# Hourglass attention and an ELU layer pair: zero matmuls through batch 0, 128-column denominator weights, and a one-element GpSimd read after each cast

## The chip, the cores and the metric

The kernel runs on one NeuronCore of a Trainium2 chip. The metric is the device time of one execution in microseconds (us). The profiled time, called the span, runs from the first to the last instruction of the program; the device time of the same execution is a little longer. Engines are named as in the profile: PE is TensorE (PEld its weight loads), DVE is VectorE, ACT is ScalarE, POOL is GpSimd, SP is SyncE, which here only issues DMAs. A suffix q (SPq, POOLq) means the engine's own instruction queue.

## The reference

Inputs are q, k and v of 8 batches x 8 heads x 576 positions x 64 in float32, and two weight matrices, w_in (512 x 2048) and w_out (2048 x 512). Each head's output is the sum of two attentions:

```python
q_d = q.reshape(B, H, Sd, 4, D).mean(axis=3)           # Sd = 144; k_d, v_d likewise
out_up = np.repeat(sm_attn(q_d, k_d, v_d), 4, axis=2)  # coarse: all 144 x 144
mask = np.abs(pos[:, None] - pos[None, :]) < 4         # local: a band of 7 keys
scores = np.where(mask, scale * q @ k.T, -1e9)
out = out_up + softmax(scores) @ v
```

The heads of a batch are put beside each other, which gives 4608 tokens of 512 values. Then h = x @ w_in, g = h where h > 0 and exp(h) - 1 elsewhere, and the result is g @ w_out, 4608 x 512 in float32.

## The kernel before

**Units.** A *pair* (b, j) is two heads of batch b, four pairs to a batch, 32 in all. A *token tile* t is 512 tokens, nine in all; a batch gives 576 tokens, so its end reaches into the next tile.

**One pair of attention.** `transposes` brings q and k to a head-dimension-first layout on PE; ACT (`evict_q` L281/L283, `evict_k` L296) copies them to SBUF. The sums over groups of four positions are made by `sums`: by DVE reductions in batch 0 (L305), by two POOL additions each in batch 1 (L311, L313), and by TensorE as part of the transposing matmul from batch 2 on. `masked_scores` (batches 0 and 1; the mask is added by a matmul, L334, then L340) or `scores` (L351, later batches) gives the local scores for six blocks of 96 queries by 112 keys, `coarse` (L361) the 144 x 144 ones. ACT exponentiates both (`pex` L372, `dex` L377). From batch 2 on, DVE multiplies by the mask (`mex`, L387). No maximum is subtracted.

**Denominators.** They are sums over keys, which lie on partitions, so they are made by matmuls with 0/1 weights. For batches 0 to 2 `den_some` does it for one or two pairs: pair i of the call writes rows 32i to 32i+31 of a PSUM bank, with 32-column weights at column position 32i (L443 seeds the bank so that no row is zero, L449 adds twelve local sums of 96 columns, L457 four coarse ones of 144). `reciprocals` inverts on DVE (L466), `spread_pe` (L476) copies each row to 64 partitions by matmul, and `spread_copy` (L485, L486) moves that to SBUF (`rcb`). Later batches do all four pairs at once (`denominators`) and spread through DRAM (`rd`).

**Output of a pair.** `outputs` (L501, L507) multiplies by v and by the four-position means of v (`vd`, by `v_first` in batches 0 and 1); `normalise` applies the reciprocals on DVE (gn L517, ln L520) and adds the two parts into the token tile xt (L529), on POOL, or for some early pieces on DVE.

**The two layers.** `mm1(t, fc)` makes 128 rows of h for a tile by four 128x512 matmuls (L545), ACT takes the exponential (`e`, L550), DVE clips it (`e`, L551) and joins it with the positive part (`gt`, L554). `mm2` multiplies by w_out (L565), ACT copies (L571), SP writes out.

**Loads and casts.** q and k of batches 0 and 1 are loaded by POOL-issued DMAs that convert to 16 bits (L152), as are w_in (WI, L139, in five column blocks) and w_out (WO, L143). q and k of later batches and all of v come by SP in float32 (L170, L193) and POOL casts them (`cast_qk` L183, `cast_v` L230); from batch 3 on POOL also makes vd from a second copy of v (`group_v`, L237 and L241).

**The order of the work.** It is written by hand. `first_batch` lists batch 0 step by step. Everything after is a list of events, `at(time, function, ...)`, sorted by time and recorded in that order; a unit of this time is one mm1/mm2 step, sixteen to a token tile. Each engine then runs its own instructions in the recorded order, and semaphores follow from the data. So a late instruction holds up all that is behind it on its engine. The numbers `base`, `tr` (transposes), `sc_` (scores), `dn` (denominators), `sp` (spreads) and `o0` (outputs) place the steps of a batch.

**PSUM.** In batch 0 there are three two-bank buffers (`two`: scores, rb, lg) and two one-bank buffers (`one`: tq, tk, vs, den, junk). Afterwards there are two of each kind: `two`, `misc` and `hp`. A tile takes the next buffer that is free, and its first writer waits for the last reader of the tile before.

**Zero matmuls.** `keep(t, n)` (L583) multiplies a zero tile by itself n times, 512 columns each, into a PSUM tile that is later overwritten. Before the change it is called twice: 14 times at the very start and twice in batch 0.

## Time and profile before

| | us |
|---|---|
| median of 3 runs (403.49 to 405.85) | 405.17 |
| the profiled execution | 404.46 |
| its span | 402.7 |
| PE busy / DVE / ACT / POOL | 369.8 / 270.3 / 206.9 / 174.4 |
| mean granted TensorE clock | 0.936 |

Busy PE is not PE at its peak: at a granted clock of 0.5 the same matmul takes about twice the time. Batch 0's attention alone fills the first 40 us. Batch 1's runs beside the first layer of token tile 0 until about 82 us; the other batches run beside the layers of tiles 1 to 7, until about 330 us. From there to the end there is only layer work. The chain that ended last is given as start, duration and what held the end of the program up at that time; in lines of the timeline the bracket at the end is the idle time of the engine before the instruction and what ended it. In lines by stretch the columns are the stretch, its length, then busy time and number of instructions of PE, PEld, DVE, ACT and POOL, the granted clock, the DMA share and GB/s.

### The profile page before, as it was taken

The page shows a single profiled execution, that of the slowest core. Times are in us where ns is not written, and L with a number is a line of the kernel's source. Part 1 is how long each engine was busy: PE and PEld are TensorE (multiplying, and loading weights), DVE is VectorE, ACT ScalarE, POOL GpSimd, SP SyncE. Part 2 cuts the span into 40 slices and gives each one's busy share as a digit, 9 for nine tenths or more (in the row PEclk, how much of TensorE's full clock was granted, in tenths as well). Part 3 has the DMA queues.
Part 4 walks back from the last instruction along what each step waited for, and adds up shares of the span by engine and source line. Part 5 has one row for each costly group of instructions (what it writes and reads, how often), then busy time and mean ns, then how long its engine had stood idle before and what let it go on. Part 6 is the DMA issues. An engine that isn't in the chain of part 4 may idle for free.

```text
span 402.7 us, 8286 instructions
## 1 busy us (share of the span) xinstructions
PE 369.8 (92%) x3244; PEld 194.6 (48%) x3244; DVE 270.3 (67%) x461; ACT 206.9 (51%) x386; POOL 174.4 (43%) x225
## 2 busy tenths in 40 slices
PE   7988999789896879988999999889999999999995
PEld 3766555445453435544544454445544444444442
DVE  3444387746747788679879886998897685555510
ACT  3442587147474456646654764566466434444321
POOL 4542872397402991089219922991490050000000
PEclk9555799989989689999999999999999999999999
DMA  8992999999976498569945994695300410100112
GB/s 137 192 208 52 145 181 145 178 163 228 201 149 116 99 188 172 137 121 227 199 127 108 222 220 131 120 234 154 77 28 28 107 55 26 48 32 26 55 52 78
DMA packets 125620, 51.99 MB, mean 129 GB/s; under 512 B 104156, under 2 KB 120974, under 8 KB 125582
## 3 DMA queue, kind: packets, MB, share of 16 engines
q1 hardware_dynamic: 116938, 44.56, 53.6%
q0 software_dynamic: 8048, 6.56, 10.9%
q8 instruction: 25, 0.41, 0.5%
q10 hardware_dynamic: 596, 0.35, 0.4%
q14 instruction: 13, 0.11, 0.1%
HBM read 48.21 MB, written 9.81 MB: 144 GB/s over the span
## 4 chain that ended last, share of the span: by engine, by line
PE 64%; DVE 18%; ACT 5%; POOL 4%; DMA 4%; issue 3%; SPq 0%; DVEq 0%; ACTq 0%; POOLq 0%
PE hp L545 24%; PE op L565 23%; DVE e L551 9%; DVE gt L554 4%; DVE ln L520 3%; PE sc L351 2%; ACT e L550 2%; POOL xt L529 2%; DMA k<-in_k_dram 2%; PE tk L269 1%; PE sc L340 1%; PE lg L501 1%; DVE mex L387 1%; DMA rd<-rc 1%; PE sc L361 1%
## 5 line engine op out<-in xcount | busy, mean ns | idle before, releaser
L545 PE MATMUL hp<-xt,WI 128*128 128x512 f16 x576 | 152.0, 389 | 4.9 <-DVE gt L554 4.8
L565 PE MATMUL op<-WO,gt 128*128 128x512 f16 x576 | 147.0, 383 | 0.7 <-DVE k L169 0.7
L550 ACT ACTIVATE e<-hp 128x512 f16<-128x512 f32 x144 | 86.2, 599 | 104.0 <-PE hp L545 100.7
L551 DVE TENSOR_SCALAR e<-e 128x512 f16<-128x512 f16 x144 | 80.1, 556 | 54.6 <-ACT e L550 53.7
L554 DVE SCALAR_TENSOR_TENSOR gt<-hp,e 128x512 f16<-128x512 f32 x144 | 99.6, 692 | 5.4
L529 POOL TENSOR_TENSOR xt<-ln,gn 128x64 f16<-128x64 f16 (+7 forms) x61 | 40.6, 693 | 131.3 <-DVE ln L520 131.3
L545 PEld LDWEIGHTS <-WI 128*128 128x128 f16 x576 | 54.0, 99 | 69.0 <-issue 11.4
L565 PEld LDWEIGHTS <-gt 128*128 128x128 f16 x576 | 54.6, 98 | 64.5 <-issue 2.7
L372 ACT ACTIVATE pex<-sc 112x576 f16<-112x576 f32 x64 | 41.4, 647 | 29.6 <-PE sc L361 19.9
L387 DVE TENSOR_TENSOR mex<-pex,MASK 112x1152 f16<-112x1152 f16 x24 | 24.7, 1030 | 14.6 <-ACT pex L372 14.6
L230 POOL CAST v<-v 112x768 f16<-112x768 f32 x32 | 27.2, 850 | 10.0 <-DMA v<-in_v_dram 10.0
L571 ACT COPY os<-op 128x512 f32<-128x512 f32 x36 | 21.2, 589 | 18.5 <-PE op L565 18.5
L237 POOL TENSOR_TENSOR v<-v 72x512 f32<-72x512 f32 x20 | 27.9, 1394 | 1.9 <-DMA v<-in_v_dram 1.8
L283 ACT CAST qt<-tq 128x720 f16<-128x720 f32 x24 | 18.1, 756 | 18.5 <-PE tq L324 11.2
L377 ACT ACTIVATE dex<-sc 72x288 f16<-72x288 f32 x64 | 25.4, 404 | 2.4 <-PE sc L361 2.4
L520 DVE TENSOR_TENSOR ln<-lg,rcb 128x576 f16<-128x576 f32 x32 | 23.9, 746 | 0.0
L183 POOL CAST k<-k 96x768 f16<-96x768 f32 x24 | 19.9, 831 | 1.4 <-DMA k<-in_k_dram 1.4
L183 POOL CAST q<-q 96x768 f16<-96x768 f32 x24 | 19.9, 829 | 1.0 <-PE tq L269 1.0
L351 PE MATMUL sc<-qt,kt 64*112 64x96 f16 x288 | 13.8, 221 | 6.4 <-DVE kd L315 4.0
L241 POOL TENSOR_TENSOR vd<-v 72x256 f16<-72x256 f32 x20 | 18.9, 943 | 1.6
L351 PEld LDWEIGHTS <-kt 64*112 64x112 f16 x288 | 10.0, 130 | 16.7 <-issue 8.4
L269 PE MATMUL tq<-QI,q 96*128 96x120 f16 x144 | 12.4, 226 | 5.3 <-POOL q L183 3.0
(83 smaller groups left out, 312.3 us busy)
## 6 DMA issues: line engine op xcount, KB each, us to landing
v<-in_v_dram SPq DMA_DIRECT2D x30, 336.0 KB
out_dram<-os SPq DMA_DIRECT2D x36, 256.0 KB
q<-in_q_dram SPq DMA_DIRECT2D x24, 288.0 KB
k<-in_k_dram SPq DMA_DIRECT2D x24, 288.0 KB
v<-in_v_dram SPq DMA_DIRECT2D x20, 288.0 KB
rcb<-rd SPq DMA_DIRECT2D x10, 288.0 KB
WO<-in_moe_w_out_dram POOLq DMA_DIRECT2D x4, 512.0 KB, 7.7
WI<-in_moe_w_in_dram POOLq DMA_DIRECT2D x3, 512.0 KB, 9.4
```

The source lines that it names most:

```text
L183: nc.gpsimd.tensor_copy(out=x[:], in_=t[:].rearrange("p (e c) d -> p c e d", e=2))
L237: nc.gpsimd.tensor_tensor(out=g[:, :, :, 0 : 2 * D], in0=g[:, :, :, 0 : 2 * D], in1=g[:, :, :, 2 * D :], op=AB.add,)
L351: nc.tensor.matmul(sc[e][0:KW, a : a + QB], s["kt"][r, QB * c : QB * c + KW], s["qt"][c][r], start=True, stop=True,)
L372: nc.scalar.activation(out=h2(s["pex"][:, e, :]), in_=g2(sc[0:KW], 0, HB), func=AF.Exp, scale=SCALE)
L387: nc.vector.tensor_tensor(out=s["mex"][:], in0=s["pex"][:], in1=mk2, op=AB.mult)
L520: nc.vector.tensor_tensor(out=h2(ln[:]), in0=g2(lg[:], 0, HB), in1=h2(rcb[:, j, 0:S]), op=AB.mult)
L529: eng.tensor_tensor(out=xt(t)[:, j, t0 - TBLK * t : t1 - TBLK * t], in0=ln[:, a:z], in1=_rep4(gn[:, a // 4 : z // 4]), op=AB.add,)
L545: nc.tensor.matmul(hp[:], WI[:, dc, 128 * fc : 128 * fc + 128], x[:, dc, :], start=(dc == 0), stop=(dc == DMC - 1),)
L550: nc.scalar.activation(out=e[:], in_=hp[:], func=AF.Exp)
L551: nc.vector.tensor_scalar(out=e[:], in0=e[:], scalar1=1.0, scalar2=-1.0, op0=AB.min, op1=AB.add)
L554: nc.vector.scalar_tensor_tensor(out=gts[t][:, fc, :], in0=hp[:], scalar=0.0, op0=AB.max, in1=e[:], op1=AB.add)
L565: nc.tensor.matmul(op_[:], gts[t][:, fc, 128 * tt : 128 * tt + 128], WO[:, fc, :], start=(fc == 0), stop=(fc == FCN - 1),)
```

## The change

Five things are changed.

1. **Zero matmuls in batch 0.** Forty 512-column zero matmuls are put between the steps of `first_batch`, in place of the two that were there: three ahead of the scores of pair 0 and four behind them, four and three behind `coarse` of pairs 0 and 1, four each between the q and the k transposes of pairs 2 and 3, three ahead of the outputs of pair 0, three ahead of `coarse` of pair 3, two each ahead of the outputs of pairs 1 to 3, and six at the end. The tiles that they write (score, rb, vs, den, lg) are allocated earlier for it.
2. **128-column weights in `den_some`.** IND and SEED are laid out anew, so that each matmul has 128 weight columns: all but one are zero in IND, and the matmuls of one pair add zeros to the rows of the other. Pairs follow each other instead of alternating. This is for batches 0, 1 and 2.
3. **`apart`.** After each cast of q, k and v of batches 2 to 7 POOL copies one element of the result into a 1x1 tile: 72 instructions.
4. **Batch 1 in another order.** Denominators are made for pairs 0 and 1 (step 7.6), 2 (11.7) and 3 (14.6) instead of for 0 and 1 (9.6), 2 and 3 (14.6). Spreads and outputs of a pair follow at once: outputs at 10.6, 11.6, 13.7 and 15.55 instead of two at 15.1 and two at 15.65. The sums of pair (1,0) are made by DVE reductions instead of POOL additions.
5. **Around batch 2's start.** Its first transposes come at -0.3 instead of 0, the casts for them 0.3 ahead instead of 0.2, and the first three loads of later q, k and v at steps 11.2, 12.2 and 13.2 instead of 11.2, 13.2 and 15.2.

In the order of each engine's instructions the rest follows from this: on POOL the casts of pair (2,0) stand before the last xt addition of batch 1, the cast of v of (1,1) and the first two WO loads one group of sums earlier; on PE one mm2 group stands behind the first transposes of batch 2 instead of ahead.

```diff
 RUNS = 2
+I1, I4 = 47, 176
 VG = 3
...
     vr[PAD + np.arange(QB), 48 + np.arange(QB) // 4] = 0.25
-    ind = np.zeros((128, 2, 63), dtype=f16)
-    ind[:, 0, 31] = 1.0
-    ind[:, 1, 31] = 4.0
-    ind = ind.reshape(128, 126)
-    seed = np.zeros((2, 64 + SD + HB), dtype=f16)
-    seed[0, 14:32] = 1.0
-    seed[1, 0:12] = 1.0
-    seed[0, 38:64] = 1.0
-    seed[1, 36:38] = 1.0
-    seed[0, 64:] = 1.0
-    seed[1, 64 + QB : 64 + SD] = 1.0
-    seed[1, 64 + 2 * SD :] = 1.0
+    ind = np.zeros((128, I4 + 63), dtype=f16)
+    ind[:, I1] = 1.0
+    ind[:, I4 + 31] = 4.0
+    seed = np.zeros((2, 288 + SD + HB), dtype=f16)
+    for n in range(2):
+        seed[0, 128 * n : 128 * n + 128] = 1.0
+        for i in range(n + 1):
+            seed[0, 128 * n + 32 * i : 128 * n + 32 * i + 14] = 0.0
+            seed[1, 128 * n + 32 * i : 128 * n + 32 * i + 12] = 1.0
+    seed[0, 262:288] = 1.0
+    seed[1, 260:262] = 1.0
+    seed[0, 288:] = 1.0
+    seed[1, 288 + QB : 288 + SD] = 1.0
+    seed[1, 288 + 2 * SD :] = 1.0
     sel = np.zeros((2, 32, 7, 2, 64), dtype=f16)
...
+    AP_ = sb.tile([1, 1], FP16, tag="apart", bufs=1, name="apart")
+    def apart(x):
+        nc.gpsimd.tensor_copy(out=AP_[:], in_=x)
     def cast_qk(b, j):
...
             nc.gpsimd.tensor_copy(out=x[:], in_=t[:].rearrange("p (e c) d -> p c e d", e=2))
+            apart(x[0:1, 0, 0, 0:1])
             got.append(x)
...
         nc.gpsimd.tensor_copy(out=v16[:], in_=v32[:].rearrange("p (e c) d -> p c e d", e=2))
+        if b >= RUNS:
+            apart(v16[0:1, 0, 0, 0:1])
         v16s[(b, j)] = v16
...
-    def transposes(b, j):
+    def transposes(b, j, fill=None):
...
             s[name] = t
+            if fill and name == "tk":
+                fill()
             for c in range(NB):
...
         src = s["q"][:, 0:S] if x == "q" else s["kt"][:, PAD : PAD + S]
-        if b == 0:
+        if b == 0 or (b, j) == (1, 0):
             nc.vector.tensor_reduce(
...
         den = bank("misc", "den")
-        o4 = 94 if b >= VG else 31
+        o4 = I4 + 31 if b >= VG else I1
         for j in range(NPAIR):
             nc.tensor.matmul(
-                den[32 * j : 32 * j + 32, 0:HB], C["SEED"][:, 32:64], C["SEED"][:, 64 + SD :],
+                den[32 * j : 32 * j + 32, 0:HB], C["SEED"][:, 256:288], C["SEED"][:, 288 + SD :],
                 start=True, stop=False, tile_position=(0, 32 * j),
...
                     nc.tensor.matmul(
-                        den[32 * j : 32 * j + 32, 0:HB], C["IND"][0:KW, 31 - r : 63 - r],
+                        den[32 * j : 32 * j + 32, 0:HB], C["IND"][0:KW, I1 - r : I1 + 32 - r],
                         st[(b, j)]["mex"][:, e, HB * g : HB * g + HB],
...
-        for i in range(len(js)):
-            nc.tensor.matmul(
-                den[32 * i : 32 * i + 32, 0:SD], C["SEED"][:, 0:32], C["SEED"][:, 64 : 64 + SD],
-                start=True, stop=False, tile_position=(0, 32 * i),
-            )
-        for r in range(12):
-            for i, j in enumerate(js):
+        n = 128 * len(js) - 128
+        nc.tensor.matmul(
+            den[:, 0:SD], C["SEED"][:, n : n + 128], C["SEED"][:, 288 : 288 + SD],
+            start=True, stop=False,
+        )
+        for i, j in enumerate(js):
+            for r in range(12):
+                a = I1 - 32 * i - r
                 nc.tensor.matmul(
-                    den[32 * i : 32 * i + 32, 0:QB], C["IND"][0:KW, 31 - r : 63 - r],
+                    den[:, 0:QB], C["IND"][0:KW, a : a + 128],
                     st[(b, j)]["mex"][:, r // 6, QB * (r % 6) : QB * (r % 6) + QB],
-                    start=False, stop=False, tile_position=(0, 32 * i),
+                    start=False, stop=False,
                 )
-        for e in range(2):
-            for kg in range(2):
-                for i, j in enumerate(js):
+            for e in range(2):
+                a = I1 - 32 * i - 12 - e
+                for kg in range(2):
                     nc.tensor.matmul(
-                        den[32 * i : 32 * i + 32, 0:SD], C["IND"][0:KG, 19 - e : 51 - e],
-                        st[(b, j)]["dex"][:, e, kg, :], start=False,
-                        stop=(e == 1 and kg == 1), tile_position=(0, 32 * i),
+                        den[:, 0:SD], C["IND"][0:KG, a : a + 128], st[(b, j)]["dex"][:, e, kg, :],
+                        start=False, stop=(j == js[-1] and e == 1 and kg == 1),
                     )
...
-    def v_first(b, j, copy=dve):
+    def v_first(b, j, copy=dve, vs=None):
-        vs = bank("misc", "vs") if late else one("vs")
+        vs = vs or (bank("misc", "vs") if late else one("vs"))
         v_sums(b, j, vs[0:KG], 128)
...
-        def T(j):
-            transposes(b, j)
+        def T(j, fill=None):
+            transposes(b, j, fill)
             evict_q(b, j, act)
...
-        def scored(j):
+        def tiles(j):
             SC[j] = [two("sc"), two("sc")]
+        def scored(j):
             for e in range(2):
...
-        def dens(js):
-            den = one("den")
+        def dens(js, den=None):
+            den = den or one("den")
             den_some(b, js, den)
...
-        def spread(j, copy):
-            rb = two("rb")
+        def spread(j, copy, rb=None):
+            rb = rb or two("rb")
             spread_pe(b, j, rb)
...
             lg = two("lg")
+            keep(lg, 2)
             outputs(b, j, lg)
...
         then()
+        tiles(0)
+        keep(SC[0][0], 3)
         scored(0)
+        tiles(1)
+        keep(SC[1][0], 4)
         T(1)
         coarsed(0)
-        keep(one("junk"), 2)
+        keep(SC[1][0], 4)
         scored(1)
-        T(2)
+        tiles(2)
+        T(2, lambda: keep(SC[2][0], 4))
         coarsed(1)
+        keep(SC[2][0], 3)
         v_first(b, 0)
...
         dens((0, 1))
-        T(3)
+        rb0 = two("rb")
+        T(3, lambda: keep(rb0, 4))
         coarsed(2)
-        spread(0, dve)
+        spread(0, dve, rb0)
         lg0 = two("lg")
+        vs = one("vs")
+        keep(vs, 3)
         outputs(b, 0, lg0)
-        v_first(b, 1)
+        v_first(b, 1, dve, vs)
+        tiles(3)
         scored(3)
         normalise(b, 0, lg0)
+        den = one("den")
+        keep(den, 3)
         coarsed(3)
         spread(1, act)
-        dens((2,))
+        dens((2,), den)
         ends(1)
...
         ends(3)
+        keep(one("junk"), 6)
         load_wi(1024, 1536)
...
-    def pair_outputs(b, j0):
-        lgs = [two("lg"), two("lg")]
-        for i in range(2):
-            outputs(b, j0 + i, lgs[i])
-        for i in range(2):
-            normalise(b, j0 + i, lgs[i])
+    def pair_outputs(b, js):
+        lgs = [two("lg") for _ in js]
+        for j, lg in zip(js, lgs):
+            outputs(b, j, lg)
+        for j, lg in zip(js, lgs):
+            normalise(b, j, lg)
...
             base, tr, sc_ = 0, (-0.1, 2.3, 6.3, 10.3), (0.3, 4.3, 8.3, 12.3)
-            dn, sp, o0 = (9.6, 14.6), (10.7, 13.6, 15.35, 15.45), (15.1, 15.65)
+            dn = ((7.6, (0, 1)), (11.7, (2,)), (14.6, (3,)))
+            sp, o0 = (8.7, 9.6, 12.8, 15.4), (10.6, 11.6, 13.7, 15.55)
         elif b == 2:
-            base, tr, sc_ = 16, (0, 3, 6, 9), (1.5, 4.5, 7.5, 10.5)
-            dn, sp, o0 = (8, 12), (9.2, 10.8, 12.6, 12.9), (13.3, 14.5)
+            base, tr, sc_ = 16, (-0.3, 3, 6, 9), (1.5, 4.5, 7.5, 10.5)
+            dn = ((8, (0, 1)), (12, (2, 3)))
+            sp, o0 = (9.2, 10.8, 12.6, 12.9), (13.3, 13.3, 14.5, 14.5)
         else:
...
             if b >= RUNS:
-                lead = 0.2 if (b, j) == (2, 0) else 3
+                lead = 0.3 if (b, j) == (2, 0) else 3
                 at(base + tr[j] - lead - 0.1, cast_qk, b, j)
...
         if b < 3:
-            for i in range(2):
-                at(base + dn[i], dens, b, (2 * i, 2 * i + 1))
+            for t, js in dn:
+                at(base + t, dens, b, js)
             for j in range(NPAIR):
                 at(base + sp[j], spread, b, j, act if j % 2 else dve)
+                at(base + o0[j], pair_outputs, b, (j,))
         else:
...
             at(base + s1, spread_in, b)
-        at(base + o0[0], pair_outputs, b, 0)
-        at(base + o0[1], pair_outputs, b, 2)
+            at(base + o0[0], pair_outputs, b, (0, 1))
+            at(base + o0[1], pair_outputs, b, (2, 3))
     at(11.1, close_runs)
     for n in range(3):
-        at(11.2 + 2 * n, load, n)
+        at(11.2 + n, load, n)
     for n in range(4):
```

More of the change, by code (lines that the diff above doesn't have):

```diff
@@ L657, in T @@
             sums(b, j, "k")
+        def tiles(j):
+            SC[j] = [two("sc"), two("sc")]
         def scored(j):
-            SC[j] = [two("sc"), two("sc")]
             for e in range(2):
```

## The prediction

> **What bounds the kernel now.** I read the page first (busy shares, the 40 slices), then busy time by stretch, then the chain that ended last in order of time, then the timeline around its longest pieces. The page names TensorE; its second row shows the granted clock.

> ```profile
> PE 369.8 (92%) x3244; PEld 194.6 (48%) x3244; DVE 270.3 (67%) x461; ACT 206.9 (51%) x386; POOL 174.4 (43%) x225
> ...
> PEclk9555799989989689999999999999999999999999
> ```

> Slices 2 to 4 (10 to 40 us) are at half clock, and single slices up to 150 us dip. The stretches of batch 0 say the same: PE is busy for 8.5 to 10 of each 10 us, at a clock near 0.50.

> ```profile
> 10.00:20.00 10.00, 9.97 (x112) 7.11 (x112) 4.48 (x7) 4.94 (x10) 5.42 (x8) 0.54 1.04 192
> 20.00:30.00 10.00, 8.53 (x98) 6.01 (x94) 4.73 (x8) 4.01 (x9) 5.00 (x8) 0.50 1.28 208
> 30.00:40.00 10.00, 8.97 (x108) 7.03 (x107) 4.75 (x8) 3.07 (x8) 2.63 (x4) 0.50 0.33 56
> ```

> The chain shows that this matters: from 15.45 to 38.99 us it is TensorE nearly without a break, and then GpSimd carries it into batch 1 (start, us, what):

> ```profile
> 19.07 1.07 PE den L449 x13
> 30.07 1.07 PE den L449 x12
> 38.11 0.62 PE lg L501 x12
> ...
> 40.23 0.80 POOL xt L529
> 41.03 0.73 POOL WI L139
> ...
> 46.45 0.45 POOL kd L313
> 46.95 0.32 PE sc L361 x4
> ```

> The third thing is in the timeline. The ELU step `e` (L551) takes 0.29 us alone, but here:

> ```profile
> 137.24 4.43 DVE L551 TENSOR_SCALAR e<-e 128x512 f16<-128x512 f16 x1 [0.20 <-ACT e L550]
> ...
> 137.61 0.82 POOL L183 CAST k<-k 96x768 f16<-96x768 f32 x1
> 138.38 0.82 POOL L230 CAST v<-v 112x768 f16<-112x768 f32 x1
> ...
> 145.64 3.02 DVE L551 TENSOR_SCALAR e<-e 128x512 f16<-128x512 f16 x1
> ```

> Six casts run from 136.85 to 141.52, each starting some 0.05 us before the one ahead ends, and `e` ends 0.15 us after the last. Where GpSimd's next instruction depends on the one before, `e` gets in between the two:

> ```profile
> 57.00 0.66 POOL L311 TENSOR_TENSOR t<-kt 128x288 f32<-128x288 f16 x1
> 57.09 0.71 DVE L551 TENSOR_SCALAR e<-e 128x512 f16<-128x512 f16 x1 [0.50 <-ACT e L550]
> ...
> 57.74 0.43 POOL L313 TENSOR_TENSOR kd<-t 128x144 f16<-128x144 f32 x1
> ```

> L311 ends at 57.66, L313 starts 0.08 later, and `e` ends at 57.80, with L313 still running.

> **Zero matmuls and the clock.** The clock changes on a grid of 3.41 us: half from 10.71 to 44.84, 82.39 to 85.80, 109.70 to 113.11, 130.18 to 137.00 and 143.83 to 147.24. For each cell I summed columns streamed, times rows/128, times weight columns/128, as a share of what a full array streams. The five full-speed cells that ended in a drop had 0.07 to 0.34, all that kept the clock 0.36 or more. At half clock, cells up to 0.52 stayed down; 0.73 and more came back. Busy time doesn't sort them. The 14 zero matmuls at the start raised the clock, so zeros count.

> The new 512-column zeros are 0.216 us each at full clock (four L565 take 0.86). In batch 0, 38 more (40 new, 2 gone) are 8.2 us. They lift the weak cell 7.30:10.71 from 0.30 to about 0.55, and by my sums no later cell of batch 0 falls under 0.45. I take full clock throughout.

> Up to 15.4 us nothing is gained. PE reaches the first v sums at 15.42 and the cast that they read ends at 15.40 (the v load lands for the cast at 14.58). At full clock with 18 zeros PE gets there at about 15.25. From there the chain holds 5.34 us of den (three times 0.23+1.07+0.48), 1.3 of ACT and 16.7 of other PE work. The same rows at full clock in batch 1 (vs 0.46 for 0.79, sc 0.69 for 1.20, transposes 0.63 for 1.31, lg 0.53 for 0.86) give a factor 0.555: 9.3 us. The new den is 3.4 (below), and 16 zeros before the last outputs 3.5. Sum 3.4+9.3+3.5+1.3 = 17.5, so PE ends at 32.9 and the last `ln` at about 34.2, not 40.16: **-6.0**. DVE's own 13.6 us of work in this stretch stay inside. Bounds: -3 if rows of DVE and ACT end more waits, -8 if most zeros fall into waits.

> **den with 128 columns.** At half clock 24 matmuls of a pair take the same 1.07 us as 12 of a single, so two 32-column blocks ran side by side; the wide ones can't. At full clock a pair takes 0.17+0.62+0.25 = 1.04. A wide one lies between 0.0405 us (0.216 x 96/512) and 0.053 (L269, 120 columns under 128 weights, 0.32 for six); with the 144-column ones at 0.061 to 0.063 a pair takes 1.5 to 1.8. I take 1.65: +0.6 a pair, and 0.85 for a single. Batch 2 has two pairs on the path: **+1.2** (0.9 to 1.5).

> **Into batch 1.** coarse(1,0) waits for GpSimd's 40.23 to 46.90. Now DVE sums (1,0) itself, two reductions of 0.745 right after its last xt. Transposes from 34.4, ACT's two evictions of 0.64, then two mm1 and two score blocks put coarse(1,0) at 38.95 instead of 47.26. That is 8.3 earlier, **-2.3** beyond the 6.0. WI's and (1,3)'s DMAs stay behind the last xt on POOL's queue, and so come 5 us earlier, with 5.5 to 9.4 us to land; WI's third quarter is wanted some 13 us later. The two WO loads that move ahead of the sums of (1,1) and (1,2) cost POOL 0.78 each, before it waits for ACT anyway.

> **Batch 1's end.** Before, den of pairs 2 and 3, two spreads, four outputs and four normalisations follow each other until POOL's cast of q at 81.52; PE idles 3.17 us before T(2,0) at 82.40. Now three pairs are done earlier, the cast of (2,0) is ahead of the last xt piece on POOL, and only pair 3's chain is left. Gone: 3.17+0.84+0.56 = 4.6 of PE gaps. New: den +0.7 and waits, since lg and rb now take PSUM buffers of `two` between score tiles: a score tile waits for rcb copies (1.05) and `ln` (1.03), about 2 us together. One mm2 group (0.86) only moves. DVE has some 30 us of work in these 36, so little more can be had. **-1.3** (-4 to +6, if every one of seven such waits costs a copy). The dip at 82.39 cost up to 1.7; with the gap gone I take **-1.0** (0 to -1.7). load(1) and load(2) come 1 and 2 steps earlier on SP, behind nothing that is late. The moved cast of q waits for load(0), which SP issues after (1,3)'s transposes; if that lands late, the cast, the next casts and the last 128-column xt piece behind it wait too, but before, issue to cast was 16 us (64.74 to 81.52), and it is some 8 now. The larger IND and SEED land long before the first den at 18.84.

> **The separators.** 72 new 1x1 copies on POOL, each waiting for the cast before it. The trace has no such row: at least 0.104 (the 128x1 memset) + 0.08 (gap at L311/L313) = 0.18; at most 0.178 (16x64 memset) + 0.08 + 0.29 (`e` ahead of it) = 0.55. Off path: POOL waits 131 us for DVE's `ln`. On path where casts stand between xt pieces (L230 at 130.90, and three later batches): **+0.8** (0 to 2).

> What they open: on the chain, `e` or `mex` blocked by casts at 137.24, 145.64, 179.51, 183.86, 189.31, 220.01, 224.59, 258.65, 264.31 and 298.00. Ending each 0.15 us (`mex` 0.62) after the first cast in its way takes 3.86 from the first and 1.54 from each other: 17.7 us of DVE. PE works on during part of it; gaps of PE right after these blocks sum to 2.57+0.58+0.70+0.96+0.86+1.42+0.85 = 7.9, and the first brings the half clock of 143.83 (1.7). The blocks at 215.01 and 293.09 stand behind xt pieces and stay. I take **-8.5**, nearest to the PE gaps; ends -5 and -17.7.

> [...]

> **Sum.** Against the profiled execution's 404.46 (0.7 under the median of 405.17): -6.0-2.3+1.2-1.3-1.0+0.8-8.5 = -17.1, so 387.4.

> **Rivals.**
> - Separators open nothing (a blocked op waits only for the cast in flight, and long ones have another cause): 404.5-9.4+0.8 = 396. Against it: the blocks at 50.85, 57.09, 182.44 and 187.48 end 0.15 us after an L311 or L237 that has a dependent instruction behind it. [...] 0.10.
> - Batch 1 turns DVE-bound on its two PSUM buffers: the -1.3 becomes +6, 394.7. For it: DVE's 30 us in 36. 0.15. Together with the first it gives 403.2, no change: 0.04.
> - The clock falls in batch 0 all the same: then 38 zeros cost 0.427 each, 16.2 us, den 1.7 more, and the 6.0 and 1.0 go: 404.5+17.9-2.3+1.2-1.3+0.8-8.5 = 412. It needs cells under 0.35 despite 0.06 per zero; it decides from about five half-clock cells (1.7 us of PE and some zeros each, against 17.1). 0.07, with 0.02 for other losses.
> - All 17.7 us of the blocks come back, and batch 0 gains 8: 376. 0.10.
> - The forecast, 380 to 394: 0.52.

> The likeliest is 387. From 376 to 399 leaves out not quite 2 in 10: 0.13 above and half of the best case below. Two us (0.5%) is about what a measurement here can tell from no change: faster 0.87, same 0.04, slower 0.09.

> **What would show it.** After: PEclk 9 in slices 2 to 4; the last `ln` of batch 0 near 34; coarse(1,0) near 39; T(2,0) near 73 without a 3 us gap; L551's mean well under 0.556 and no `e` over 2 us except behind xt pieces; 72 copies of about 0.1 us. Wrong if half clock persists under the zeros, if `e` still spans several casts, or if score tiles of batch 1 wait for rcb or `ln` by microseconds.

## The result and the profile after

The changed kernel takes 393.14 us (median of 4 runs, 391.39 to 393.68), the kernel before 405.14 beside it: a ratio of 0.970, with a 95% interval of 0.966 to 0.975. It is faster by 12.0 us; 18.2 (405.17 - 387.0) had been forecast. The profiled execution, the shortest of the four, took 391.39 us, 13.07 less than the one of before, where the sum had given 17.1.

From the page of the changed kernel: busy time of the engines, the granted clock in 40 slices, the chain that ended last by engine, and the ELU step `e`, which is now line 565.

```profile
PE 366.6 (94%) x3278; PEld 191.0 (49%) x3278; DVE 259.5 (67%) x464; ACT 206.6 (53%) x386; POOL 185.3 (48%) x293
...
PEclk9999999999899899989999999999999999999999
...
PE 69%; DVE 13%; DMA 6%; ACT 5%; issue 3%; POOL 2%; SPq 2%; DVEq 0%; ACTq 0%
...
L565 DVE TENSOR_SCALAR e<-e 128x512 f16<-128x512 f16 x144 | 66.7, 463 | 51.7 <-ACT e L564 50.6
```

The half clock of slices 2 to 4 is gone, three single cells later (101.90 to 105.32, 125.80 to 129.21 and 166.76 to 170.17 in the trace's clock; a cell is 3.41 us, the grid on which its changes stand in both traces) are all that is left of it, and `e` has come down from a mean of 556 ns to 463. These were the two main steps of the forecast. DMA's share of the chain has gone from 4% to 6%.

The stretches of batch 0, in the columns of the page (PE, PEld, DVE, ACT, POOL, then the granted clock, DMA share, GB/s):

```profile
10.00:20.00 10.00, 10.00 (x137) 6.51 (x136) 4.94 (x8) 5.56 (x11) 4.80 (x7) 1.00 0.90 168
20.00:30.00 10.00, 10.00 (x150) 6.30 (x147) 6.33 (x11) 4.78 (x11) 5.62 (x9) 1.00 1.30 208
30.00:40.00 10.00, 9.89 (x131) 5.91 (x130) 6.65 (x12) 5.24 (x12) 7.20 (x11) 1.00 0.63 104
```

The timeline shows what a separator does (L186 is the 1x1 copy, L192 a cast of q or k):

```profile
130.39 0.81 POOL L192 CAST q<-q 96x768 f16<-96x768 f32 x1
...
130.49 0.86 DVE L565 TENSOR_SCALAR e<-e 128x512 f16<-128x512 f16 x1
...
131.26 0.18 POOL L186 COPY apart<-q 1x1 f16<-1x1 f16 x1
131.39 0.69 DVE L568 SCALAR_TENSOR_TENSOR gt<-hp,e 128x512 f16<-128x512 f32 x1
131.39 0.82 POOL L192 CAST k<-k 96x768 f16<-96x768 f32 x1
```

The cast ends at 131.20, the copy that needs its result starts 0.06 later, and `e` ends at 131.35, 0.15 after the one cast that was in its way. The copy's record is 0.18 us, the lower bound of the forecast; where DVE got in ahead of it, the record is 0.80.

How far ahead the changed kernel is, by the start of ACT's `e` of the same rows of h in both traces (us; fc counts the sixteen steps of a token tile):

| step | before | after | ahead by |
|---|---|---|---|
| tile 0, fc 4 | 51.08 | 43.70 | 7.38 |
| tile 1, fc 0 | 86.23 | 78.00 | 8.23 |
| tile 1, fc 12 | 121.75 | 115.05 | 6.70 |
| tile 2, fc 0 | 136.61 | 129.45 | 7.16 |
| tile 2, fc 4 | 150.49 | 138.30 | 12.19 |
| tile 3, fc 0 | 180.60 | 171.99 | 8.62 |
| tile 4, fc 0 | 219.38 | 208.01 | 11.38 |
| tile 6, fc 0 | 297.37 | 284.12 | 13.26 |
| tile 8, fc 12 | 378.82 | 365.80 | 13.02 |

Five us are won within four steps of tile 2, where before the six casts stood in the way of one `e`, and 3.6 of them are lost again by the start of tile 3. The chain of waits shows what stands there (start, us, what):

```profile
147.93 1.29 DVE mex L401
...
150.98 4.01 DMA rd<-rc
...
157.05 3.96 DMA rcb<-rd
161.01 0.03 issue
...
161.43 0.76 DVE ln L534
162.19 0.07 issue
162.26 2.64 POOL xt L543 x4
164.90 1.28 POOL v L249
```

The reciprocals of batch 3 go out to DRAM (`rd`) and come back spread over the partitions (`rcb`), and DVE's first normalisation waits for them: 2.28 us there, 2.75 at 237.9 and 0.67 at 274.5. In the waits of the tile `rcb`, the time in which its readers sat idle for its DMA, and how often, is

```profile
  DMA rcb<-rd: 5.7, 3
```

Before, DVE waited 1.4 us for it in all, and the trip stood on the chain once (from 237.14); now it stands there at 150.98 and 227.18, and with its way back alone at 269.38. So the theory at this point: the casts' chains are open as forecast, and most of what they gave is eaten by this trip through DRAM, which is next in line. The rival: the separators are worth little, and the gain of 5 us in tile 2 is the clock's (before, it was at half from 143.83 to 147.24; after, it was at full from 129.22 to 166.76).

### The profile page after: what moved, and what is told of

It is laid out like the page before. It is cut to its first block, busy times and chain, and to the rows that moved or that the text cites. A ratio compares the mean times of both kernels' runs of the same rounds, so it can differ in the third digit from the quotient of the medians.

```text
span 389.6 us, 8427 instructions
## 1 busy us (share of the span) xinstructions
PE 366.6 (94%) x3278; PEld 191.0 (49%) x3278; DVE 259.5 (67%) x464; ACT 206.6 (53%) x386; POOL 185.3 (48%) x293
## 4 chain that ended last, share of the span: by engine, by line
PE 69%; DVE 13%; DMA 6%; ACT 5%; issue 3%; POOL 2%; SPq 2%; DVEq 0%; ACTq 0%
PE op L579 25%; PE hp L559 24%; DVE e L565 4%; DMA rcb<-rd 4%; DVE gt L568 3%; DVE ln L534 3%; PE sc L597 3%; PE sc L365 2%; DMA rd<-rc 2%; PE tk L283 2%; POOL xt L543 2%; PE sc L354 1%; PE den L464 1%; SPq L445 1%; ACT e L564 1%
## 5 line engine op out<-in xcount | busy, mean ns | idle before, releaser
L559 PE MATMUL hp<-xt,WI 128*128 128x512 f16 x576 | 150.8, 386 | 1.0 <-DVE gt L568 0.9
L565 DVE TENSOR_SCALAR e<-e 128x512 f16<-128x512 f16 x144 | 66.7, 463 | 51.7 <-ACT e L564 50.6
L559 PEld LDWEIGHTS <-WI 128*128 128x128 f16 x576 | 53.7, 99 | 62.3 <-issue 3.5
L240 POOL CAST v<-v 112x768 f16<-112x768 f32 x32 | 26.4, 825 | 9.9 <-DMA v<-in_v_dram 9.9
L249 POOL TENSOR_TENSOR v<-v 72x512 f32<-72x512 f32 x20 | 25.8, 1289 | 1.3 <-DMA v<-in_v_dram 1.3
L192 POOL CAST q<-q 96x768 f16<-96x768 f32 x24 | 19.9, 829 | 0.6 <-PE tq L283 0.6
L192 POOL CAST k<-k 96x768 f16<-96x768 f32 x24 | 19.6, 817 | 0.0
L253 POOL TENSOR_TENSOR vd<-v 72x256 f16<-72x256 f32 x20 | 16.3, 814 | 1.6
L531 DVE TENSOR_TENSOR gn<-lg,rcb 128x144 f16<-128x144 f32 x32 | 9.6, 301 | 10.3 <-DMA rcb<-rd 5.7
L515 PEld LDWEIGHTS <-v 112*64 112x64 f16 x384 | 10.4, 109 | 12.1 <-DVE ln L534 5.7
L310 ACT CAST kt<-tk 128x576 f16<-128x576 f32 x24 | 15.6, 652 | 0.4
```

The lines of the kernel that those rows point to most:

```text
L192: nc.gpsimd.tensor_copy(out=x[:], in_=t[:].rearrange("p (e c) d -> p c e d", e=2))
L240: nc.gpsimd.tensor_copy(out=v16[:], in_=v32[:].rearrange("p (e c) d -> p c e d", e=2))
L249: nc.gpsimd.tensor_tensor(out=g[:, :, :, 0 : 2 * D], in0=g[:, :, :, 0 : 2 * D], in1=g[:, :, :, 2 * D :], op=AB.add,)
L559: nc.tensor.matmul(hp[:], WI[:, dc, 128 * fc : 128 * fc + 128], x[:, dc, :], start=(dc == 0), stop=(dc == DMC - 1),)
L565: nc.vector.tensor_scalar(out=e[:], in0=e[:], scalar1=1.0, scalar2=-1.0, op0=AB.min, op1=AB.add)
```

## Experiments

Each is told by its ratio to the kernel before, run beside it; one hundredth of a ratio is 4.05 us. The difference of two such ratios is known to some 2 to 3 us, by their 95% intervals.

### The separators: alone, left out, and without their wait

The kernel before with nothing but the separators:

```diff
...
             nc.gpsimd.tensor_copy(out=x[:], in_=t[:].rearrange("p (e c) d -> p c e d", e=2))
+            apart(x[0:1, 0, 0, 0:1])
             got.append(x)
...
```

By the theory the separators alone bring the 5.9 us by which the lead in the table grows from fc 0 of tile 2 to fc 12 of tile 8 (7.16 to 13.02), where casts ran against DVE: 399 us, with a mean of `e` under 500 ns.

> The kernel before with the separators alone: one 1x1 copy behind every cast of q, k and v of batches 2 to 7, nothing else changed. [...] Rival (the separators open nothing; the 5.9 came from the new order): 405, or 406 with what the copies cost. Second rival (they need the clock and order of the changed kernel, as DVE is late in another place otherwise): 402 to 405 with L551's mean down all the same.

Measured: 403.65 us, ratio 0.993 (0.989 to 0.998): 2.8 us faster, not quite half of the 5.9 that the rows had promised. `e`'s mean falls to 485 ns all the same, so the second rival is nearest: the blocks open, and the time goes elsewhere. The trace shows a part of where: the readers of `rcb` wait 8.6 us for its DMA in this kernel, in two gaps, and 1.4 us in the kernel before.

The changed kernel without them:

```diff
-            apart(x[0:1, 0, 0, 0:1])
...
-        if b >= RUNS:
-            apart(v16[0:1, 0, 0, 0:1])
```

> The changed kernel without the separators, all else kept. Theory: the 5.9 us come back, 393.1 + 5.9 = 399, between 397 and 401; e of the layers again spans several casts (3 to 4.5 us) at some ten places. Rival (separators open nothing): 392 to 393.5.

Measured: 395.88 us, ratio 0.976 (0.974 to 0.979), 2.5 us slower than with them (0.976 against 0.970); less than both traces had let expect, and not far above what the ratios can tell from nothing (2.0 us). The 5 us won within tile 2 are not the clock's: here it is at full from 131.20, and from fc 0 (130.09) to fc 4 (143.66) of tile 2 this kernel gains 0.31 us on the one before, where the changed kernel gains 5.03. Its timeline has the long block back: one `e` spans six casts, and ends 0.15 us after the last (line numbers are three lower; L239 casts v):

```profile
130.72 4.12 DVE L562 TENSOR_SCALAR e<-e 128x512 f16<-128x512 f16 x1 [0.51 <-ACT e L561]
...
133.87 0.82 POOL L239 CAST v<-v 112x768 f16<-112x768 f32 x1
134.66 1.29 POOL L246 TENSOR_TENSOR v<-v 72x512 f32<-72x512 f32 x1
134.87 0.69 DVE L565 SCALAR_TENSOR_TENSOR gt<-hp,e 128x512 f16<-128x512 f32 x1
```

The readers of `rcb` hardly wait for the DMA here:

```profile
  DMA rcb<-rd: 0.3, 1
```

Is it the copy's wait, or just an instruction of another shape between two casts? The changed kernel with copies of a constant, whose only wait is for the copy before, long done:

```diff
-        nc.gpsimd.tensor_copy(out=AP_[:], in_=x)
+        nc.gpsimd.tensor_copy(out=AP_[:], in_=C["SEL"][0:1, 0:1])
```

> The changed kernel with separators of the same size and number that copy an element of a constant instead of one of the cast's result, so they need not wait for the cast ahead of them. If GpSimd's wait for the end of its own cast is what lets DVE in: as without separators, 397 to 401. If an instruction of another shape behind the cast is enough: as the changed kernel, 392.5 to 394.

Measured: 434.12 us, ratio 1.071 (1.070 to 1.073). Both theories missed: it is 41 us slower than with the wait, and 38 slower than with no copies at all. The timeline of the same place:

```profile
133.55 0.81 POOL L192 CAST q<-q 96x768 f16<-96x768 f32 x1
...
133.66 6.68 DVE L565 TENSOR_SCALAR e<-e 128x512 f16<-128x512 f16 x1
...
134.32 0.18 POOL L186 COPY apart<-SEL 1x1 f16<-1x1 f16 x1
...
134.44 0.82 POOL L192 CAST k<-k 96x768 f16<-96x768 f32 x1
...
138.80 0.18 POOL L186 COPY apart<-SEL 1x1 f16<-1x1 f16 x1
138.94 1.25 POOL L249 TENSOR_TENSOR v<-v 72x512 f32<-72x512 f32 x1
140.27 0.72 POOL L253 TENSOR_TENSOR vd<-v 72x256 f16<-72x256 f32 x1
```

Here `e` is held across six casts, six copies and the addition L249, and ends (140.34) 0.15 after that addition; L253, which reads what L249 wrote, starts 0.08 after it. So an instruction in between opened nothing here (6.68 us, against 4.12 across the bare casts); GpSimd having to wait for its own result did (0.86). It is not the only thing that did: without copies DVE got in where the last cast gave way to an addition that reads none of the casts' results, and with idle copies there it did not, so the hold became longer. Why that is so, no run here shows. DVE is busy with `e` for 102.1 us (709 ns each), against 66.7 in the changed kernel and 80.0 without copies. The 22 us more than without copies are not the whole of the 38; half clock, which is back in twelve cells after 85 us (the mean is 0.953, against 0.986), was not separated from them.

### The trip through DRAM

The changed kernel, with the transfers into `rcb` reading a constant, so that they need not wait for the landing of `rd` (the normalisation of batches 3 to 7 is left out by this):

```diff
...
+    RD["ones"] = nc.inline_tensor(np.ones((128, HB), dtype=np.float16), name="onesc").ap()
...
     def spread_in(b):
-        rd = RD[b]
+        rd = RD["ones"]
...
```

> The changed kernel, except that the reciprocals of batches 3 to 7 are spread from a constant of ones in DRAM: the transfer has the same size and place in the queues, but it need not wait for the landing of the one that writes the reciprocals (left out: the normalisation of batches 3 to 7; the denominators, the reciprocals and their write are still made). Theory (the round trip through DRAM, three times on the chain of the changed kernel with some 8 to 10 us each and gaps of TensorE of about 4.0, 1.3 and 1 us, has taken the place of the casts): 393.1 - 3 to -6, so 387 to 390. Rival (it is level with other work, mostly DVE's steps and GpSimd's additions to xt): 392.5 to 393.5.

Measured: 389.10 us, ratio 0.959 (0.955 to 0.963): 4.6 us faster than the changed kernel, as the theory said. The trip is shorter here and not gone: the readers of `rcb` still wait 4.2 us for its DMA (0.45 ahead of 156.90 and 3.76 ahead of 233.28), against 5.7. To see whether this is the separators' missing share, and not a gain that any kernel would have, the same edit in the kernel without separators:

> The changed kernel with neither the separators nor the wait for the reciprocals' landing (spread from constant ones in batches 3 to 7, whose normalisation is left out). With the changed kernel, the one without separators (2.4 us slower by the ratios) and the one without the wait (4.6 us faster) it completes a square. Theory (the round trip took what the separators had opened): without the separators nothing waits for the round trip, as the chain of that kernel has no DMA in it, so this runs as it did, 394.5 to 396.5, and the separators are worth 5 to 7 us where the round trip is out of the way. Rival (the two add up): the wait is worth 4.6 us here too, 391 to 392.

Measured: 396.37 us, ratio 0.977 (0.974 to 0.981), no faster than with the wait. The square, in ratios:

| | waits for `rd` | does not wait |
|---|---|---|
| separators | 0.970 | 0.959 |
| none | 0.976 | 0.977 |

Where `rcb` does not wait for `rd`, the separators are worth 0.018, 7.4 us; where it does, 2.5. And that wait costs 4.6 us with them and nothing without. The one difference less the other is 4.9 us, known to 3.0, and that settles it for the theory: each hides the other. Can the clock have made these differences? Its mean over the four runs is 0.981 in the changed kernel, 0.988 without the separators, 0.988 without the wait and 0.986 without both. From 0.986 to 0.988 is some 2 us less at half clock, by my estimate about 1 us of TensorE's work (a zero takes 0.427 us at half clock and 0.216 at full), so hardly any of the 7.4 is the clock's. Of the 4.6, up to 2.8 can be half clock that goes with the wait (0.981 against 0.988); that was not separated.

Part of the trip is SP's queue. The reciprocal of batch 3 (145.81, 1.95 us long) was ready at 147.76, and its DMA was issued at 150.98, behind these (SP's issues):

```profile
145.15 1.18 SPq L173 DMA_DIRECT2D k<-in_k_dram  x1
146.42 2.32 SPq L203 DMA_DIRECT2D v<-in_v_dram  x1
148.83 1.60 SPq L229 DMA_DIRECT2D v<-in_v_dram  x1
150.52 0.37 SPq L587 DMA_DIRECT2D out_dram<-os  x1
150.98 0.38 SPq L438 DMA_DIRECT2D rd<-rc  x1
```

### The zero matmuls and what the clock goes by

Without the 40 zeros of batch 0 (`keep` makes only the 14 at the start):

> The changed kernel without the 40 zero matmuls in batch 0 (the 14 at the start stay), all else kept. Theory: half clock in batch 0 as before the change, and the 6.0 us of the zeros gone, with perhaps 1 us at the dip at 82 us: 393.1 + 5 to 8 = 398 to 401. Rival (the other changes had carried the gain, as a later clock change or the new order of batch 1 takes up what batch 0 loses): 392 to 395.

Measured: 401.46 us, ratio 0.990 (0.985 to 0.994): the zeros are worth 7.9 us. The clock is at half from 17.03 to 47.75 in the trace.

With zeros of the same length on a part of the array, first 32 of 128 weight columns:

```diff
...
-            nc.tensor.matmul(t[:, 0:w], Z[:, 0:128], Z[:, 0:w], start=True, stop=True)
+            nc.tensor.matmul(
+                t[0:cols, 0:w], Z[:, 0:cols], Z[:, 0:w], start=True, stop=True,
...
```

> The changed kernel with the 40 zero matmuls of batch 0 at 32 weight columns instead of 128 (the 14 at the start stay): the same 512 columns streamed, so the same busy time, over a quarter of the array. Theory (the clock goes by the share of the array in use): the cells of batch 0 fall to the 0.07 to 0.35 at which the clock dropped before, and it is half for most of 10 to 40 us; the zeros and everything else there take twice as long, so some 8 to 17 us more, 401 to 410. Rival (the clock goes by TensorE's busy time): full clock and 392.5 to 394.5.

Measured: 392.82 us, ratio 0.970 (0.965 to 0.976), the same as with whole zeros, and full clock throughout batch 0 (1.00 from 10 to 40 us). My measure, the share of the array in use, falls: four cells of batch 0 had 0.28 to 0.33 of it here and kept the clock, where before the change 0.07 to 0.34 had lost it. Then 32 columns and 32 of 128 rows (the lines that differ from the edit above):

```diff
-                t[0:cols, 0:w], Z[:, 0:cols], Z[:, 0:w], start=True, stop=True,
+                t[0:cols, 0:w], Z[0:cols, 0:cols], Z[0:cols, 0:w], start=True, stop=True,
```

> The changed kernel with the 40 zero matmuls of batch 0 cut to 32 rows and 32 weight columns (a sixteenth of the array; the 14 at the start stay), 512 columns streamed each as before. With 32 columns and all 128 rows the clock had held, with cells at 0.28 to 0.35 of the array. If the rows carry it (columns streamed times rows, the width counting for nothing): cells of batch 0 lose up to 0.4 and the clock drops for most of 10 to 44 us, 400 to 410. If it is TensorE being busy, in whatever part of the array: full clock, 392 to 394.

Measured: 412.16 us (two runs), ratio 1.018 (1.009 to 1.028), slower than before the change. By stretch, the kernel with 128 rows and the one with 32:

```profile
10.00:20.00 10.00, 10.00 (x141) 6.47 (x140) 4.48 (x7) 5.08 (x10) 5.24 (x8) 1.00 0.95 183
20.00:30.00 10.00, 10.00 (x148) 6.29 (x148) 6.67 (x11) 4.96 (x11) 5.18 (x8) 1.00 1.29 211
```

```profile
10.00:20.00 10.00, 10.00 (x88) 4.83 (x87) 4.03 (x7) 4.10 (x9) 5.00 (x7) 0.62 0.92 176
20.00:30.00 10.00, 10.00 (x90) 6.84 (x89) 2.44 (x4) 2.39 (x4) 4.11 (x7) 0.50 1.29 207
```

The last full-speed cell of the kernel with 32 rows, after which the clock dropped, was busy from end to end:

```profile
9.00:12.41 3.41, 3.41 (x44) 1.79 (x44) 2.21 (x4) 2.32 (x5) 0.00 (x0) 1.00 0.97 174
```

TensorE is busy for all of the time in both (10.00 of 10.00 us), and the clock is 1.00 in one and 0.50 in the other. So in these runs it isn't busy time, and it isn't the array's share: the rows count (412.16 us against 392.82 at the same 32 columns), and the width counts for much less than its share (392.82 with 32 columns, 393.14 with 128). Over the full-speed cells of all fourteen profiled executions (1,224 up to 330 us, 51 of which lost the clock), the best threshold misplaces 17 by columns streamed, 13 if each column counts rows/128, 12 by TensorE's busy time, 11 by the share of the array, and 5 if each column counts rows/128 times (1/4 + 3/4 of the width). That last rule is my estimate, fitted to these traces after the fact, and zeros with few rows and full width were not tried. The changes of the clock stand on a grid of 3.41 us whose phase differs from run to run: before the change it was at full from 3.88 and at half from 10.71 to 44.84, two and then ten cells; after it at full from 6.33 and first at half from 101.90, 28 cells later.

### The other parts, each undone alone

Denominators of batches 0 to 2 with 32-column weights again (`den_some` as before the change):

> The changed kernel with 32-column denominator weights in batches 0 to 2, as before the change. Theory (the wide ones cost 0.75 us a pair and 4 pairs lie on the path outside of batch 0, and the clock holds without them): 393.1 - 1.5 to -3, so 390 to 391.5. Rival (the wide weights are part of what holds the clock: a den stretch at 32 columns has a quarter of the array share): half clock in one or two cells of batches 0 to 2, 393 to 397.

Measured: 391.30 us, ratio 0.966 (0.963 to 0.970): the wide weights cost 1.7 us, which the ratios alone cannot tell from nothing (they know it to 2.3), and the clock holds in batch 0 without them (its mean in the profiled execution is 0.981; without the zeros it was 0.943). The cost is plain in the timeline of batch 2's first call: first wide (changed kernel: twelve local sums of one pair, its four coarse ones, then the next pair's twelve), then with narrow weights (all twenty-four local sums, two beside each other, in the 0.69 us of twelve):

```profile
94.96 0.69 PE L464 MATMUL den<-mex,IND 112*128 112x96 f16 x12
95.48 0.41 PE L472 MATMUL den<-dex,IND 72*128 72x144 f16 x4
95.73 0.68 PE L464 MATMUL den<-mex,IND 112*128 112x96 f16 x12
```

```profile
93.91 0.69 PE L463 MATMUL den<-mex,IND 112*32 112x96 f16 x24
```

The order of batch 1 as before the change (and with it the first transposes and casts of batch 2):

```diff
...
-            dn = ((7.6, (0, 1)), (11.7, (2,)), (14.6, (3,)))
-            sp, o0 = (8.7, 9.6, 12.8, 15.4), (10.6, 11.6, 13.7, 15.55)
+            dn = ((9.6, (0, 1)), (14.6, (2, 3)))
+            sp, o0 = (10.7, 13.6, 15.35, 15.45), (15.1, None, 15.65, None)
...
```

> The changed kernel with denominators, spreads and outputs of batch 1 where they were before the change (and batch 2's first transposes and casts too); the sums of pair (1,0) stay on VectorE and the earlier loads stay. My prediction gave the new order -1.3 us, the trace of after +0.1 (a gain of 3.1 us at the start of batch 2 lost to score tiles that wait 0.5 to 1.2 us each for PSUM). If the trace's reading holds: 392 to 394. If the order is worth what was predicted or more, because the old one brings back the 3 us gap and the clock's dip behind it: 395 to 398.

Measured: 396.19 us, ratio 0.979 (0.973 to 0.984): the new order is worth 3.4 us, and the reading that I had from the trace, +0.1, falls. Its timeline has the gap of before ahead of batch 2, and behind it the matmuls at half clock (75.51 to 82.33; four of L559 take 1.91 us, and 1.04 at full clock):

```profile
76.14 0.78 PE L283 MATMUL tq<-QI,q 96*128 96x120 f16 x6 [3.00 <-POOL q L192]
...
78.74 1.91 PE L559 MATMUL hp<-xt,WI 128*128 128x512 f16 x4
```

The sums of pair (1,0) on GpSimd again:

```diff
-        if b == 0 or (b, j) == (1, 0):
+        if b == 0:
```

> The changed kernel with the sums of pair (1,0) made by GpSimd's additions again, as before the change. My prediction gave their move to VectorE 2.3 us. The four other parts, each undone alone, were worth -7.9 (zeros), -3.4 (order of batch 1), +1.7 (wide weights) and -2.5 (separators) by the ratios, which is already all of the -12.0. If the parts are independent, the move is worth nothing: 392.5 to 394. If the 2.3 are real and are given back later in the changed kernel (the parts overlap): 394.5 to 396.

Measured: 397.06 us, ratio 0.979 (0.973 to 0.985): 3.5 us, so the second theory. In the trace `e` of tile 0 goes from 0.50 ahead of the changed kernel (fc 0) to 3.72 behind it (fc 4); a cell of half clock from 42.88 to 46.29 is in that, which can hold up to 1.7 of it.

The five parts undone one by one give 7.9 + 3.5 + 3.4 + 2.5 - 1.7 = 15.6 us, where all of them together gave 12.0. The 3.6 by which the sum is over the whole are within the noise: the changed kernel's own ratio, known to 0.004, stands in it four times over, and with the others' errors the difference is known to 8 us.

### A faster version

The changed kernel with 32-column denominators and, in batches 3 to 7, the last pairs' transposes and scores, the denominators and the trip through DRAM earlier; outputs and casts stay, and so do the loads, but for some of `load_groups` that move with `group_v` by 0.2 to 0.4 of a step:

```diff
...
-            base, tr, sc_ = start_of(b) - 26.5, (0, 3.2, 9.7, 12.9), (1.6, 4.8, 11.3, 14.5)
-            d0, s0, s1, o0 = 16.1, 17.7, 18.7, (22.5, 24.1)
+            base, tr, sc_ = start_of(b) - 26.5, (0, 3.2, 9.3, 12), (1.6, 4.8, 10.9, 13.4)
+            d0, s0, s1, o0 = 14.8, 16.2, 17.2, (22.5, 24.1)
...
-                base, tr, sc_ = start_of(b) - 22, (0, 3.2, 6.4, 9.6), (1.6, 4.8, 8, 11.2)
-                d0, s0, s1, o0 = 12.8, 14, 15, (19, 20.6)
+                base, tr, sc_ = start_of(b) - 22, (0, 3, 5.8, 8.5), (1.6, 4.4, 7.2, 9.9)
+                d0, s0, s1, o0 = 11.3, 12.6, 13.6, (19, 20.6)
...
```

> A version meant to be faster: the changed kernel with 32-column denominator weights (391.3 in their own run), and in batches 3 to 7 the transposes and scores of the last pairs, the denominators and the trip of the reciprocals through DRAM 0.9 to 1.6 steps (2 to 3.5 us) earlier, outputs where they were; casts and loads stay. If the trip is late by 1 to 4 us and no more, as TensorE's gaps say: most of the 4.6 us that taking its wait away gave come back, 391.3 - 2.5 to -4.5 = 387 to 389. If the earlier scores only move the wait into the PSUM buffers that scores and outputs share: 390.5 to 392.

Measured: 385.53 us (383.66 to 386.75), ratio 0.954 (0.947 to 0.960), faster than both kernels and a little faster than expected. The page has no DMA on the chain any more, and one cell of half clock is left:

```profile
PE 361.4 (95%) x3282; PEld 187.1 (49%) x3282; DVE 257.0 (67%) x464; ACT 206.0 (54%) x386; POOL 184.3 (48%) x293
...
PEclk9999999999998999999999999999999999999999
...
PE 78%; DVE 12%; ACT 5%; issue 2%; POOL 1%; DVEq 0%; ACTq 0%
```

The readers of `rcb` do not wait for its DMA any more. Against the kernel with narrow weights alone (0.966) the earlier steps together gave 5.1 us, known to 3.2: about what taking the wait away had given (4.6), and without leaving anything out. The mean granted clock over the runs rises from 0.981 to 0.992, so up to 4.4 of the 5.1 can be half clock that no longer comes; what the trip and what the earlier scores gave was not separated.

## Why the prediction was right in kind and 6 us short

- **Batch 0, -6.0: right.** From the first v sums to the transposes of pair (1,0) it was 24.85 us (15.45 to 40.30) and is 18.79 (16.84 to 35.63): 6.1 less by the starts in the two chains, at full clock all through. What the sum did not hold is the start: the grid's phase gave the first full clock at 6.33 us instead of 3.88, so the 14 first zeros took 5.71 us instead of 4.50, and the first v sums came 1.4 late. The zeros start at 1.20 us in both, so I put that down to the execution's luck, not to the change. With it the last `ln` ends at 35.35 (34.2 forecast, 40.16 before).
- **Its reason was wrong in one point.** That the clock goes by the share of the array sorted the cells of one trace and fell with the 32-column zeros (392.82 us, clock 1.00). The forecast came out all the same, as the new zeros had all the rows and the full width. The rival "the clock falls in batch 0 all the same", priced at 412, was built by taking rows and width away, and ran at 412.16. That the two agree is luck in part: the price held -8.5 for the casts. The loss itself was put at 24.6 us (412 less 387.4) and is 19.4 by the ratios (1.018 against 0.970).
- **Into batch 1, -2.3: right.** `coarse` of pair (1,0) ends at 39.88 (38.95 forecast) instead of 47.26; 7.4 earlier, of which 2.7 are beyond the 4.7 by which the transposes of (1,0) are early. Undone alone: 3.5.
- **Wide denominators, +1.2: right.** The lead falls from 8.23 to 6.70 over batch 2, with one cell of half clock in each trace there; undone alone 1.7. A call for two pairs (the prediction's "pair") takes 1.70 us, from its first matmul to the next instruction behind it, and with narrow weights 1.04; 1.65 and 1.04 were taken.
- **Batch 1's end and the dip, -1.3 and -1.0: too small.** By the trace the first transposes of batch 2 are 7.3 early, no earlier than `coarse` of (1,0), because TensorE does wait for DVE in between: score tiles for `rcb` copies (0.55 ahead of 54.33, 0.40 ahead of 65.06), a spread behind the reciprocals (0.58 ahead of 63.22) and an mm2 behind the copy of `vd` (0.96 ahead of 71.24). That looked like +0.1. But the old order would have lost more on the earlier start, 3 us of gap and two cells at half clock: undone alone the part is worth 3.4, against 2.3 for the two terms.
- **The separators' price, +0.8 on the path: not seen in itself.** The copies take 0.18 us, as bounded from below, and no xt piece on the chain waits behind one.
- **The casts' chains opened, -8.5: the step that failed.** "Ending each 0.15 us after the first cast in its way" is what the timeline shows, and the size was sound: with the copies' price 7.7 net, and 7.4 was measured where `rcb` does not wait for `rd`. But the whole of it was put into the sum, and only 2.5 came. The five other terms hold as a sum: they give 9.4, and the kernel without separators gains 9.6 by its ratio. This step needed an answer to what is late next, and the prediction gave none: the denominators' trip through DRAM, which the chain of before had once already, at 237.14, with 1.4 us of waits, is not shortened when `e` gets faster, and its wait took 4.6 us of the gain.
- **"The blocks at 215.01 and 293.09 stay": right.** They are at 206.94 (2.07 us) and 283.02 (2.22), behind an xt piece and L249.
- **The rivals.** "Separators open nothing", 396, is not what happened, but its price was good: the kernel without them runs at 395.88 (395.1 is the rival's sum without the copies' 0.8). "Batch 1 turns DVE-bound" did not come: its order gained. "All 17.7 us come back" did not come either: 7.4 was the most that was measured.
- **A row of casts, not one, held `e`: right.** It took 4.12 us across six casts without separators, 0.86 with them, and 6.68 with copies that need not wait.

## What to carry to other kernels

When a stall off TensorE is taken away, look in the trace of before for the longest fixed delay between the same two points (here a write to DRAM and its way back, some 13 us from the reciprocal to the first use: 147.76 to 161.21 in the changed kernel): it has slack that is not on the chain, and that slack bounds the gain (here 2.5 us came of 7.4). To find two causes that hide each other, build all four kernels: from the one without separators, these alone gave 2.5 us, the wait taken away alone gave none, and the two together gave 7.1. Where a row of independent casts on GpSimd held VectorE up here (4.12 us for one `e`), one small instruction that had to wait for the one before let VectorE in (0.86); one that need not wait made it worse (6.68).
